# Layer 1 keeps scales and turned quarters of a weight for layer 2, which makes only the sums

## The chip, the cores and the metric

One core of a Trainium2 chip runs the whole program in one launch. The metric is the device time of one execution in microseconds (us); smaller is better. Besides the timed runs there is one profiled execution of the same program, from which all rows below come.

## The reference, cut to what matters

Two attention layers and two gated MLP layers follow each other: `x = x + A(ln(x))`, `x = x + B(ln(x))`, and both once more with the same weights. The change lies in the two B layers, here called layer 1 and layer 2:

```python
def _B_ref(x, w_in, w_sp, b_sp, w_out):            # S = 2048 rows, D = 640, F = 1728, Fh = 864
    z = _gelu(jnp.einsum("bsd,df->bsf", x, w_in))
    z1 = z[..., :Fh]
    z2 = _layernorm(z[..., Fh:], axis=-1)
    g = jnp.einsum("ts,bsf->btf", w_sp, z2) + b_sp[None, :, None]
    return jnp.einsum("bsf,fd->bsd", z1 * g, w_out)
```

`w_sp` (2048 x 2048) multiplies over the sequence, so its rows must be turned (transposed) before TensorE can use them. Both layers use the same `w_sp`.

## The kernel before, in words

All matrix products work on pairs of 16-bit numbers (a high half and the rest, `h` and `l`), three matmuls for one product. A row of `w_sp` is first scaled by a power of two that its largest element gives, then split into `h` and `l` and turned by a transposing DMA.

**Layer 1's spatial product** is in `phase2`. For each of 16 row tiles `t` (128 rows), `rows(t)` loads the 1 MB tile `wr` (one buffer), finds each row's maximum (L577) and scale (`pow2_rows`), and, for each half of the columns, casts the high half on ACT (L587), subtracts on DVE (L588) and turns the result into `wt` by a DMA from the SP queue (L589; two buffers of `wt`). `spatial(t)` runs 96 matmuls over the 16 column blocks (L600) and prepares `u`, which is split and turned to `ut` (L616). `tail` multiplies `ut` by the output weight (`cyp`, L629). TensorE's order is that of the code; a list scheduler sets the order on the other engines and on SP in this phase.

**Layer 2's spatial product** is in `phase2s`. It takes the tiles in eight pairs (256 rows) and cuts the pair's 2 x 2 blocks into quarters a11, a12, a21, a22; seven products of quarter sums replace eight. The sums of `z2` (`zb[0]` to `zb[6]`) are there before. For the weight, `rows(p)` loads the pair's two tiles `wr` (two buffers, L417), finds maximum and scale (L419, `pow2`), scales in place on ACT (L424), and yields seven turned operands in the order in which TensorE uses them: a11, s1 = a21 + a22, s2 = s1 - a11, a12, s3 = a11 - a21, a22, s4 = a12 - s2. The four sums run on POOL (`mix`, L441). Each operand is cast (L431), subtracted (L432) into one of two `wn` buffers and turned (512 KB, L435) into one of eight `wt` buffers. After each product `step` fetches the next operand of the generator, seven ahead.

One pair on TensorE: seven products of 24 matmuls (L458) into the banks `ga` to `gd`, and between them two `tail`s (42 matmuls, `cyp`, L494) of the pair before. After the last product of a tile, `gate` multiplies by `z1` (L473), finds the row maximum (L475), splits on ACT and DVE into the single buffer `un` (L479, L480) and turns it to `ut` (L482). A `tail` waits for that `ut`; its output `xo` (L497) is stored from SP (L498). In `phase2s` both TensorE's and SP's instructions stand in the order of the code; ACT, DVE and POOL are ordered by the scheduler. SP issues every DMA of the kernel, one after the other, and an issue that waits holds back all that stand behind it.

Of the kernel before, what the change touches and what calls it, by code (L numbers as in the profile page):

```python
# [387 lines left out]
def phase2s(g, w_sp, x1_d, z1_d, zb, w0, out):  # L388
# [3 lines left out]
    RING = 8  # L392
    kn = [128] * 6 + [FH - 768]
    ks = [0, 1, 2, 3, 6, 7, 4, 5]
    with ExitStack() as ctx:
        pool = lambda n, b, **k: ctx.enter_context(tc.tile_pool(name=n, bufs=b, reuse_waits="tile", **k))
        pr, ph, ps = pool("dr", 2), pool("dh", 2), pool("ds", 2)
        p1, p2, pv = pool("d1", 1), pool("d2", 2), pool("dv", 1)
        pt = pool("dtr", 1, side="right")
# [3 lines left out]
        cnt, scales = [0], {}  # L403
# [8 lines left out]

        def rows(p):
            w = []
            for t in (2 * p, 2 * p + 1):
                wr = pr.tile([128, S], F32, tag="wr", name="wr")
                nc.sync.dma_start(wr, w_sp[t * 128:(t + 1) * 128, :])  # L417
                am = small("am")
                nc.vector.tensor_reduce(am, wr, AX.X, ALU.max, apply_absolute_value=True)  # L419
                pw, iv = pow2(am, "w", WB)  # L420
                u = g.small.tile([128, 1], F32, tag=f"un{t % 2}", name="un")
                scales.setdefault(p, []).append(u)
                nc.vector.tensor_scalar(u, pw, 1.0 / (WB * ZB), None, ALU.mult)
                nc.scalar.activation(wr, wr, AF.Identity, scale=iv)  # L424
                v = wr.rearrange("p (m i c) -> p i m c", i=2, c=128)
                w.append((v[:, 0], v[:, 1]))

            def turned(src):
                hl = ph.tile([128, 2, 1024], F16, tag="wn", name="wn")
                v = hl.rearrange("p l (m c) -> p l m c", c=128)  # L430
                nc.scalar.copy(v[:, 0], src)  # L431
                nc.vector.tensor_tensor(v[:, 1], src, v[:, 0], ALU.subtract)  # L432
                wt = pt.tile([128, 2, NP, 128], F16, tag=f"wt{cnt[0] % RING}", name="wt")
                cnt[0] += 1
                nc.sync.dma_start(wt.rearrange("p l k c -> p (l k) c"), hl.rearrange("p l c -> p (l c)"), transpose=True)  # L435
                return wt

            def mix(a, b, op, o=None):
                if o is None:
                    o = ps.tile([128, 1024], F32, tag="s", name="s").rearrange("p (m c) -> p m c", c=128)  # L440
                nc.gpsimd.tensor_tensor(o, a, b, op)  # L441
                return o

            (a11, a12), (a21, a22) = w
            yield turned(a11)
            s1 = mix(a21, a22, ALU.add)
            yield turned(s1)
            s2 = mix(s1, a11, ALU.subtract)
            yield turned(s2)
            yield turned(a12)  # L450
            yield turned(mix(a11, a21, ALU.subtract, a21))
            yield turned(a22)
            yield turned(mix(a12, s2, ALU.subtract, a12))
# [7 lines left out]
        def scaled(o, a, un, t):  # L461
            nc.scalar.activation(o, a[:, :FHH], AF.Identity, bias=g.bsp[:, t:t + 1], scale=un)

        def plus(o, a, un, b):
            nc.vector.scalar_tensor_tensor(o, a[:, :FHH], un, b, ALU.mult, ALU.add)
# [6 lines left out]
        def gate(t, u, z1):  # L472
# [4 lines left out]
            hl = p1.tile([128, 2, 128 * KO], F16, tag="un", name="un")  # L477
# [9 lines left out]
        def tail(t, uh, ul, xs, x1=None):  # L487
# [8 lines left out]
            xo = p1.tile([128, 2, 320], F32, tag="xo", name="xo")  # L496
# [3 lines left out]
        todo = (o for p in range(NP) for o in rows(p))  # L500
        with tc.high_priority(offset=HP), ExitStack() as held:
            for i in g.mark:
                held.enter_context(tc.issue_after(i))
            wt = [next(todo) for _ in range(7)]
# [4 lines left out]
        for p in range(NP):  # L509
# [4 lines left out]
            pa, pb, pc, pd = [bank(nm) for nm in "abcd"]  # L514
# [6 lines left out]
            un, un1 = scales[p]  # L521
            step(pa, 0)
            scaled(v, pa, un, t)
            scaled(v1, pa, un1, t + 1)
# [8 lines left out]
            step(pa, 1, False)  # L533
            scaled(u[:, :FHH], pa, un, t)
            step(pb, 5, False)
            plus(q1, pb, un1, v1)
            plus(u1[:, FHH:], pc, un1, q1)
            x1 = [fetch("x1", i, x1_d[i]) for i in (t + 1, t)[:1 + (p + 1 < NP)]] + [None]
            step(pd, 6)
            plus(u1[:, :FHH], pd, un1, q1)  # L540
            pend.append((*gate(t + 1, u1, z1[0]), x1[0]))
            step(pc, 2, False)
            plus(u[:, FHH:], pc, un, q)
            pend.append((*gate(t, u, z1[1]), x1[1]))
        for x in pend:
            tail(*x)


def phase2(g, w_sp, x1_d, z1_d, zh, zl, out, nxt=None):
# [3 lines left out]
    with ExitStack() as ctx:  # L553
# [19 lines left out]
        def rows(t):  # L573
# [4 lines left out]
            pw, iv = pow2_rows(am, "w")  # L578
            un = g.small.tile([128, 1], F32, tag="un", name="un")
            nc.vector.tensor_scalar(un, pw, 1.0 / (WTOP * ZS), None, ALU.mult)  # L580
            ivw = g.small.tile([128, 1], F32, tag="wivw", name="ivw")
            nc.vector.tensor_scalar(ivw, iv, WTOP, None, ALU.mult)
# [829 lines left out]
def interleaved_layers(ctx, tc, x, wq, wk, wv, wo, beta, w_in, w_sp, b_sp, w_out, out):  # L1412
# [68 lines left out]
```

## Time and profile before

| what | value |
|---|---|
| time, median of 3 runs | 2458.88 us (2454.61 to 2461.70) |
| time of the profiled execution | 2444.19 us |
| its span in the profile | 2442.3 us |
| TensorE busy (PE) | 2198.3 us, 90% of the span, 20490 matmuls |
| VectorE (DVE), ScalarE (ACT), GpSimd (POOL) busy | 1554.6, 1197.7, 1066.6 us |
| layer 1's `phase2` on TensorE, first and last spatial matmul | 847.0 to 1233.4 us |
| layer 2's `phase2s` on TensorE, first matmul to last tail | 2016.8 to 2438.2 us |

The profiled execution's time is its span and 1.9 us around it. A row of the timeline has the start, the duration, the engine, the line, the operation, the tiles written and read, the count of merged instructions, and in brackets the idle time of that engine before it and what ended that idle time. PE is TensorE's matmuls, SPq the SP queue's DMA issues. A matmul's recorded duration overlaps the next one's, so that 24 matmuls recorded as 4.54 us follow each other every 4.38 us. Rows of waits have the sum, the count and the longest.

### The profile page before, as it was taken

The page shows a single profiled execution, that of the slowest core. Times are in us where ns is not written, and L with a number is a line of the kernel's source. Part 1 is how long each engine was busy: PE and PEld are TensorE (multiplying, and loading weights), DVE is VectorE, ACT ScalarE, POOL GpSimd, SP SyncE. Part 2 cuts the span into 40 slices and gives each one's busy share as a digit, 9 for nine tenths or more (in the row PEclk, how much of TensorE's full clock was granted, in tenths as well). Part 3 has the DMA queues.
Part 4 walks back from the last instruction along what each step waited for, and adds up shares of the span by engine and source line. Part 5 has one row for each costly group of instructions (what it writes and reads, how often), then busy time and mean ns, then how long its engine had stood idle before and what let it go on. Part 6 is the DMA issues. An engine that isn't in the chain of part 4 may idle for free.

```text
span 2442.3 us, 50615 instructions
## 1 busy us (share of the span) xinstructions
PE 2198.3 (90%) x20490; PEld 1305.8 (53%) x20490; DVE 1554.6 (64%) x2869; ACT 1197.7 (49%) x1476; POOL 1066.6 (44%) x787
## 2 busy tenths in 40 slices
PE   5788899999899899999988989999989987798888
PEld 2454555666455455555544556565655543455454
DVE  7678778776745455444236787887667674555663
ACT  4378688787622322111125987887764242223221
POOL 2178778888510000000004988897863242112320
PEclk9989899999999999999999999999999998899999
DMA  5644545445634488575333263554644327776774
GB/s 164 163 136 102 130 119 137 131 123 146 185 98 128 134 211 199 156 177 145 80 97 89 82 172 100 130 111 127 174 124 114 102 73 182 178 195 151 169 191 106
DMA packets 552426, 337.58 MB, mean 138 GB/s; under 512 B 458432, under 2 KB 493376, under 8 KB 547072
## 3 DMA queue, kind: packets, MB, share of 16 engines
q1 hardware_dynamic: 552192, 334.35, 53.1%
q8 instruction: 161, 2.64, 0.4%
q14 instruction: 73, 0.60, 0.1%
HBM read 148.25 MB, written 85.34 MB: 96 GB/s over the span
## 4 chain that ended last, share of the span: by engine, by line
PE 24%; DMA 8%; DVE 7%; ACT 5%; issue 3%; POOL 2%; SPq 1%; ACTq 0%; DVEq 0%; POOLq 0%
PE zp L308 6%; DMA wt<-wn 2%; PE cyp L494 2%; PE pv L1222 2%; PE yps L979 2%; PE kps L1003 1%; PE gb L458 1%; DMA ut<-un 1%; DVE wn L432 1%; PE mp L1169 1%; PE qps L1003 1%; ACT PH L1195 1%; ACT P L1178 1%; DMA wr<-in_B_w_sp_dram 1%; PE vps L946 1%
## 5 line engine op out<-in xcount | busy, mean ns | idle before, releaser
L1196 POOL TENSOR_TENSOR PL<-P,PH 128x1280 f16<-128x1280 f32 x248 | 650.1, 2623 | 111.3 <-ACT PH L1195 99.6
L1185 DVE TENSOR_REDUCE mx<-mp 128x2 f32<-128x1024 f32 (+3 forms) x512 | 408.8, 817 | 103.9 <-PE mp L1141 102.4
L1178 ACT ACTIVATE P<-es,sc 128x1024 f32<-128x1024 f32 (+1 forms) x384 | 370.7, 965 | 133.0 <-PE es L1141 130.7
L1195 ACT CAST PH<-P 128x1280 f16<-128x1280 f32 x256 | 320.4, 1253 | 20.0 <-PE pv L1222 12.7
L308 PEld LDWEIGHTS <-th 128*128 128x128 f16 x1920 | 187.5, 98 | 176.1 <-issue 8.2
L600 PE MATMUL gp<-zh,wt 128*128 128x432 f16 x1024 | 235.2, 350 | 10.6 <-DMA wt<-wn 10.6
L211 POOL TENSOR_TENSOR lnrs<-lnve,mhalf 128x1 f32<-128x1 f32 x92 | 56.7, 625 | 409.8 <-DVE lnve L210 389.2
L600 PEld LDWEIGHTS <-wt 128*128 128x128 f16 x1536 | 151.8, 99 | 143.8 <-DMA wt<-wn 11.4
L458 PEld LDWEIGHTS <-wt 128*128 128x128 f16 x1344 | 133.4, 99 | 153.3 <-issue 25.2
L1169 PEld LDWEIGHTS <-qk 60*128 60x128 f16 (+1 forms) x2048 | 91.3, 94 | 226.3 <-issue 152.5
L1169 PE MATMUL mp<-qk 60*128 60x512 f16 (+3 forms) x1024 | 138.4, 307 | 42.6 <-DVE mx L1185 41.5
L1222 PE MATMUL pv<-vs,PH 128*128 128x41 f16 x2560 | 167.4, 182 | 1.7 <-DVE ab L1238 1.6
L1141 PEld LDWEIGHTS <-big 64*128 64x128 f16 x3072 | 141.5, 96 | 50.6 <-issue 2.9
L946 PE MATMUL vps<-wvh,xt 128*128 128x320 f16 x640 | 155.6, 310 | 14.0 <-DMA xt<-xnhl 12.0
L1169 PE MATMUL es<-qk 64*128 64x512 f16 (+3 forms) x1024 | 135.1, 299 | 34.9 <-ACT P L1178 23.9
L1222 PE MATMUL pv<-vs,PL 128*128 128x41 f16 x2560 | 163.5, 181 | 1.6 <-POOL PL L1196 1.6
L308 PE MATMUL zp<-wi1h,th 128*128 128x432 f16 x640 | 149.4, 348 | 4.4 <-DMA th<-xnhl 4.3
L1222 PEld LDWEIGHTS <-PH 128*128 128x128 f16 x2560 | 142.3, 96 | 18.6
L615 POOL MEMSET un<- 128x64 f16 x16 | 2.4, 152 | 335.9 <-DMA ut<-un 295.5
L1222 PEld LDWEIGHTS <-PL 128*128 128x128 f16 x2560 | 143.1, 97 | 3.8 <-POOL PL L1196 2.1
L600 PE MATMUL gp<-zl,wt 128*128 128x432 f16 x512 | 137.6, 351 | 0.0
L494 PE MATMUL cyp<-w,ut 128*128 128x320 f16 (+1 forms) x672 | 103.4, 318 | 36.0 <-DMA ut<-un 33.5
(249 smaller groups left out, 4623.4 us busy)
## 6 DMA issues: line engine op xcount, KB each, us to landing
wr<-in_B_w_sp_dram SPq DMA_DIRECT2D x32, 1024.0 KB
qk<-st SPq DMA_DIRECT2D x256, 120.0 KB
x<-x SPq DMA_DIRECT2D x56, 320.0 KB
z<-z SPq DMA_DIRECT2D x32, 432.0 KB
cz<-z SPq DMA_DIRECT2D x32, 432.0 KB
st<-qhl SPq DMA_DIRECT2D x40, 256.0 KB
st<-khl SPq DMA_DIRECT2D x40, 256.0 KB
cx<-x SPq DMA_DIRECT2D x32, 320.0 KB
```

Source lines behind the costliest of these rows:

```text
L308: nc.tensor.matmul(zp[:, n, :FHH], a[:, k, :], b[:, k, c:c + FHH], start=(k == 0 and j == 0), stop=(k == KD - 1 and j == 2))
L458: nc.tensor.matmul(o[:, :FHH], wt[:, x, m, :], zb[b][:, y, m, :], start=start and i == j == 0, stop=i == NP - 1 and j == 2, skip_group_che ...
L494: nc.tensor.matmul(yp[:, n, :320], a[:kn[k], k, :], b[:kn[k], k, n * 320:(n + 1) * 320], start=(k == 0 and j == 0), stop=(k == KO - 1 and ...
L600: nc.tensor.matmul(gp[:, n, :FHH], wt[:, k // 8, a, k % 8, :], b[:, k, n * FHH:(n + 1) * FHH], start=(k == 0 and j == 0), stop=(k == NT - ...
L946: nc.tensor.matmul(ps, a[:, k, c], b[:, k, n * 320:(n + 1) * 320], start=(i == 0), stop=(i == 14))
L1141: nc.tensor.matmul(out, g.big[r, 64 - 64 * s:192 - 64 * s], mk, start=False, stop=s == 1, skip_group_check=True)
L1169: nc.tensor.matmul(out[:, h, o:o + w], a[r, ac], b[r, bc], start=o == 0, stop=False, skip_group_check=True)
L1178: self.last_of["ACT"] = nc.scalar.activation(P[:, :, 512 * c:512 * c + ew], es[:, :, :ew], AF.Exp, scale=g.esc).ins
L1185: self.last_of["DVE"] = nc.vector.tensor_reduce(self.mx[m][:, :, i], mp[:, :, o:o + w], AX.X, ALU.max).ins
L1195: nc.scalar.copy(PH, P[:, h])
L1196: (nc.gpsimd if h == 0 or n < self.N - self.TAIL else nc.vector).tensor_tensor(PL, P[:, h], PH, ALU.subtract)
L1222: nc.tensor.matmul(pv[:, i, h, :], x[:, c:c + 128], v[:, j, h0 + h, :], start=(j == 0 and x is PH), stop=(j == i and x is PL), skip_group_ ...
```

## The change

Layer 1 scales with layer 2's factor (`WB` instead of `WTOP`), splits the columns by alternating blocks of 128 (as layer 2's quarters lie) instead of by halves, keeps each row's scales in the tiles `wpw` and `wiv` (two small POOL copies for each tile), and after each `spatial(t)` stores the turned quarters that layer 2 needs unsummed to DRAM tensors `turned`: both of an even tile (a11, a12), the second of an odd one (a22), 24 stores of 512 KB. Layer 2 finds no maxima and scales any more. It loads a11, a12 and a22 turned from DRAM by plain DMAs, and casts, subtracts and turns only the four sums. `make(n)` makes the operand `n`, `turn(n)` issues its DMA, five operands ahead in a ring of six. `wr` has three buffers, and `rows(p + 1)` is issued after the first product of pair `p`. `un` has two buffers. The seventh product has its own bank `ge`, and its result is added to `u` by a second pass; the two tails stand one product later.

```diff
-    RING = 8
+    RING, AHEAD = 6, 5
-        pr, ph, ps = pool("dr", 2), pool("dh", 2), pool("ds", 2)
+        pr, ph, ps = pool("dr", 3), pool("dh", 2), pool("ds", 2)
...
         def rows(p):
-            w = []
-            for t in (2 * p, 2 * p + 1):
-                wr = pr.tile([128, S], F32, tag="wr", name="wr")
-                nc.sync.dma_start(wr, w_sp[t * 128:(t + 1) * 128, :])
-                am = small("am")
-                nc.vector.tensor_reduce(am, wr, AX.X, ALU.max, apply_absolute_value=True)
-                pw, iv = pow2(am, "w", WB)
...
+            for t in (2 * p + 1, 2 * p):
+                raw[t] = pr.tile([128, S], F32, tag="wr", name="wr")
+                nc.sync.dma_start(raw[t], w_sp[t * 128:(t + 1) * 128, :])
+
+        def scale(p):
+            for t in (2 * p + 1, 2 * p):
+                wr = raw.pop(t)
+                nc.scalar.activation(wr, wr, AF.Identity, scale=g.wiv[:, t:t + 1])
...
+        def make(n):
+            p, b = divmod(n, 7)
+            if p >= NP or b in (0, 3, 5):
+                return
+            if b == 1:
+                scale(p)
+                (a11, a12), (a21, a22) = mixed[2 * p], mixed[2 * p + 1]
+                mixed[p, 1] = src = mix(a21, a22, ALU.add)
...
+            hl = ph.tile([128, 2, 1024], F16, tag="wn", name="wn")
+            v = hl.rearrange("p l (m c) -> p l m c", c=128)
+            nc.scalar.copy(v[:, 0], src)
+            nc.vector.tensor_tensor(v[:, 1], src, v[:, 0], ALU.subtract)
+            split[n] = hl
+
+        def turn(n):
+            p, b = divmod(n, 7)
...
+            wt = pt.tile([128, 2, NP, 128], F16, tag=f"wt{n % RING}", name="wt")
+            if b in (0, 3, 5):
+                nc.sync.dma_start(wt.rearrange("p l k c -> p (l k c)"), g.turned[2 * p + (b == 5)][b > 0])
+            else:
+                nc.sync.dma_start(wt.rearrange("p l k c -> p (l k) c"), split.pop(n).rearrange("p l c -> p (l c)"), transpose=True)
...
-            hl = p1.tile([128, 2, 128 * KO], F16, tag="un", name="un")
+            hl = p2.tile([128, 2, 128 * KO], F16, tag="un", name="un")
...
-            def step(o, b, start=True):
-                product(o, wt.pop(0), b, start)
-                wt.extend(islice(todo, 1))
+            def step(i, o, b, start=True):
+                n = 7 * p + i
+                product(o, ready.pop(n), b, start)
+                turn(n + AHEAD)
+                if i == 0:
+                    rows(p + 1)
+
+            def then(i):
+                make(7 * p + i + AHEAD + 1)
...
-            step(pc, 3)
-            if pend:
-                tail(*pend.pop(0))
-            step(pb, 4)
-            plus(q, pb, un, v)
+            step(1, pc, 3)
+            then(1)
+            step(2, pb, 4)
+            plus(q, pb, t, v)
+            plus(u[:, FHH:], pc, t, q)
+            then(2)
+            if pend:
+                tail(*pend.pop(0))
+            step(3, pa, 1, False)
+            scaled(u[:, :FHH], pa, t)
+            then(3)
             if pend and p + 1 < NP:
                 tail(*pend.pop(0))
...
-            step(pc, 2, False)
-            plus(u[:, FHH:], pc, un, q)
+            step(6, pe, 2)
+            plus(u[:, FHH:], pe, t, u[:, FHH:])
             pend.append((*gate(t, u, z1[1]), x1[1]))
+            then(6)
...
+        def store(t, wt):
+            for i in range(t % 2, 2):
+                nc.sync.dma_start(g.turned[t][i], wt[0][:, i].rearrange("p l k c -> p (l k c)"))
...
-                        nc.tensor.matmul(gp[:, n, :FHH], wt[:, k // 8, a, k % 8, :], b[:, k, n * FHH:(n + 1) * FHH],
+                        nc.tensor.matmul(gp[:, n, :FHH], wt[:, k % 2, a, k // 2, :], b[:, k, n * FHH:(n + 1) * FHH],
...
             u = spatial(t, wt)
+            store(t, wt)
             wt = rows(t + 1) if t + 1 < NT else None
```

Three places show how the instructions stand now. The first is SP in layer 2, from the loads of the next pair's rows to the first `ut` of the running pair: before,

```order
L417 DMA wr<-in_B_w_sp_dram 128x2048 x2
L435 DMA_TRANSPOSE wt<-wn 128x16x128 x2
L498 DMA out_dram<-xo 128x640
L435 DMA_TRANSPOSE wt<-wn 128x16x128
L498 DMA out_dram<-xo 128x640
L469 DMA cz_30374<-z_1_9 128x864
L469 DMA cz_30376<-z_1_8 128x864
L435 DMA_TRANSPOSE wt<-wn 128x16x128 x2
L469 DMA cx_30440<-x_1_9 128x640
L469 DMA cx_30442<-x_1_8 128x640
L435 DMA_TRANSPOSE wt<-wn 128x16x128
L482 DMA_TRANSPOSE ut<-un 128x14x128
```

and the same stretch now (the first turned operand is s4 of the running pair, the next two s1 and s2 of the next pair):

```order
L422 DMA wr<-in_B_w_sp_dram 128x2048 x2
L467 DMA_TRANSPOSE wt<-wn 128x16x128
L465 DMA wt<-turned_0 128x2048
L513 DMA out_dram<-xo 128x640
L467 DMA_TRANSPOSE wt<-wn 128x16x128
L513 DMA out_dram<-xo 128x640
L484 DMA cz_30302<-z_1_9 128x864
L484 DMA cz_30304<-z_1_8 128x864
L467 DMA_TRANSPOSE wt<-wn 128x16x128
L484 DMA cx_30334<-x_1_9 128x640
L484 DMA cx_30336<-x_1_8 128x640
L465 DMA wt<-turned_1 128x2048
```

Behind it follow `ut`, the turned s3, the second `ut` and a plain load of a22, and then the next `wr`: three of seven transposing DMAs became plain loads, and the second output's store now stands between s1 and s2.

The second place is DVE in a middle pair, from the splits (`wn`) to the first gate (`u<-u,cz`): before,

```order
L432 TENSOR_TENSOR wn<-wr,wn 128x1024
L432 TENSOR_TENSOR wn<-s,wn 128x1024 x2
L465 SCALAR_TENSOR_TENSOR q_30548<-gb,un,v_30546 128x432
L465 SCALAR_TENSOR_TENSOR u<-gc,un,q_30548 128x432
L497 SCALAR_TENSOR_TENSOR xo<-cyp,xs,cx_30442 128x640
L432 TENSOR_TENSOR wn<-wr,wn 128x1024
L465 SCALAR_TENSOR_TENSOR u<-gd,un,q_30548 128x432
L432 TENSOR_TENSOR wn<-wr,wn 128x1024
L473 TENSOR_TENSOR u<-u,cz_30761 128x864
```

and now:

```order
L456 TENSOR_TENSOR wn<-s,wn 128x1024 x2
L456 TENSOR_TENSOR wn<-wr,wn 128x1024
L512 SCALAR_TENSOR_TENSOR xo<-cyp,xs,cx_30336 128x640
L480 SCALAR_TENSOR_TENSOR q_30440<-gb,unt,v_30438 128x432
L480 SCALAR_TENSOR_TENSOR u<-gc,unt,q_30440 128x432
L456 TENSOR_TENSOR wn<-wr,wn 128x1024
L480 SCALAR_TENSOR_TENSOR u<-gd,unt,q_30440 128x432
L488 TENSOR_TENSOR u<-u,cz_30662 128x864
```

The third split (s3, `wn<-wr`) stands ahead of the second `xo`, and the fourth (s4) ahead of `u<-gd`, with which the first gate of the pair begins.

The third place is ACT where layer 2's first pair begins: before,

```order
L431 CAST wn<-s 128x1024
L431 CAST wn<-wr 128x1024 x2
L462 ACTIVATE v<-ga,bsp,un 128x432
L462 ACTIVATE v_28703<-ga,bsp,un 128x432
L431 CAST wn<-wr 128x1024 x2
```

(a11 and s1 were cast further up), and now:

```order
L363 CAST zb_26770<-zt_28604 128x432
L477 ACTIVATE v<-ga,bsp,unt 128x432
L477 ACTIVATE v_28730<-ga,bsp,unt 128x432
L455 CAST wn<-s 128x1024 x2
L455 CAST wn<-wr 128x1024 x2
```

All four casts of the first pair stand behind `v`, which reads the first product.

More of the change, by code (lines that the diff above doesn't have):

```diff
@@ L411, in pow2 @@
             return pw, iv
+        un = g.small.tile([128, NT], F32, tag="unt", name="unt")
+        nc.vector.tensor_scalar(un, g.wpw, 1.0 / (WB * ZB), None, ALU.mult)
+        un = [un[:, t:t + 1] for t in range(NT)]
+        raw, mixed, split, ready = {}, {}, {}, {}
         def rows(p):
[L414 to L426 removed]
@@ L438, in mix @@
[L438 to L450, printed above, removed]
@@ L451, in rows @@
-            yield turned(mix(a11, a21, ALU.subtract, a21))
-            yield turned(a22)
-            yield turned(mix(a12, s2, ALU.subtract, a12))
+            if p >= NP:
+                return
[6 more added lines that the diff above has]
+                nc.scalar.activation(wr, wr, AF.Identity, scale=g.wiv[:, t:t + 1])
+                v = wr.rearrange("p (m i c) -> p i m c", i=2, c=128)
+                mixed[t] = v[:, 0], v[:, 1]
@@ L503, in phase2s @@
                 held.enter_context(tc.issue_after(i))
-            wt = [next(todo) for _ in range(7)]
+            rows(0)
+            for n in range(AHEAD + 1):
+                make(n)
+                if n < AHEAD:
+                    turn(n)
         woh, wol = g.wu.place(w0)
@@ L1417, in interleaved_layers @@
     g.bsp = cp.tile([128, NT], F32, tag="bsp", name="bsp")
+    g.wpw = cp.tile([128, NT], F32, tag="wpw", name="wpw")
+    g.wiv = cp.tile([128, NT], F32, tag="wiv", name="wiv")
     attn_consts(g, cp, beta)
@@ L1428, in interleaved_layers @@
     g.st = [dram(f"st{i}", (D, 3, 2, L), F16) for i in range(2)]
+    g.turned = [[dram(f"turned{t}_{i}", (128, 2048), F16) for i in range(2)] for t in range(NT)]
     kept = kept_tiles(g, ats)
```

77 lines of the change are left out of this document (43 added, 34 removed).

## The prediction

> **What bounds the kernel now.** I read the stages first (busy times of the engines in windows), then who TensorE waits for in the last stage, then its timeline there, and last the other engines' rows in one pair. Layer 1's spatial stage, once under way, from the windows; the columns are the window, its length, the busy times of PE, weight load, DVE, ACT, POOL, the clock, the DMA share and GB/s:
>
> ```profile
> 892.00:1233.00 341.00, 337.75 (x2014) 197.34 (x2012) 143.23 (x256) 61.88 (x64) 9.88 (x22) 0.99 0.61 149
> ```
>
> PE is busy for 337.75 of 341 us at 0.99 of full clock: TensorE bounds this stage, and whatever delays it there is lost for good. Layer 2's stage (2016 to 2443) is different. PE's waits there (sum in us, times, longest):
>
> ```profile
> PE cyp L494 <- DMA ut<-un: 33.5, 6, 13.2
> PE ga L458 <- DMA wt<-wn: 19.0, 2, 14.4
> PE gc L458 <- DVE u L465: 14.5, 8, 4.3
> ```
>
> Together 67 us: the tails wait for the gate's turned `ut`, and pairs 0 and 1 for their turned a11. PE's timeline shows where:
>
> ```profile
> 2006.60 5.64 PE L308 MATMUL zp<-w,th 128*128 128x432 f16 x30
> 2016.84 6.08 PE L458 MATMUL ga<-zb,wt 128*128 128x432 f16 x24 [4.60 <-DMA wt<-wn]
> 2022.76 4.54 PE L458 MATMUL gc<-zb,wt 128*128 128x432 f16 x24
> 2027.13 4.54 PE L458 MATMUL gb<-zb,wt 128*128 128x432 f16 x24
> 2044.65 4.54 PE L458 MATMUL gc<-zb,wt 128*128 128x432 f16 x24
> 2063.59 6.59 PE L458 MATMUL ga<-zb,wt 128*128 128x432 f16 x24 [14.39 <-DMA wt<-wn]
> 2087.73 7.79 PE L494 MATMUL cyp<-w,ut 128*128 128x320 f16 x42 [13.17 <-DMA ut<-un]
> 2099.73 5.87 PE L494 MATMUL cyp<-w,ut 128*128 128x320 f16 x42
> 2197.71 5.87 PE L494 MATMUL cyp<-w,ut 128*128 128x320 f16 x42
> 2228.91 4.54 PE L458 MATMUL gc<-zb,wt 128*128 128x432 f16 x24 [1.68 <-DVE u L465]
> 2237.78 7.55 PE L494 MATMUL cyp<-w,ut 128*128 128x320 f16 x42 [4.33 <-DMA ut<-un]
> 2289.00 7.84 PE L494 MATMUL cyp<-w,ut 128*128 128x320 f16 x42 [5.21 <-DMA ut<-un]
> 2389.14 7.27 PE L494 MATMUL cyp<-w,ut 128*128 128x320 f16 x42 [4.59 <-DMA ut<-un]
> 2400.64 4.54 PE L458 MATMUL ga<-zb,wt 128*128 128x432 f16 x24
> 2432.36 5.87 PE L494 MATMUL cyp<-w,ut 128*128 128x320 f16 x42 [1.49 <-DVE xo L497]
> ```
>
> A product takes 2027.13 - 2022.76 = 4.37 us, a tail 5.71 (5.87 as recorded, less the overlap of 0.16), so a pair is 7 x 4.37 + 2 x 5.71 = 42.0 us of TensorE. But the first tails of pairs 1 and 7 begin 2389.14 - 2087.73 = 301.4 us apart, 50.2 a pair. From 2237.78 on the wait in each pair is 4.3 to 5.2 us, and it costs more than itself: that tail is recorded as 7.55 to 7.84 us and not 5.87, some 1.7 us at a lower clock. After 1.68 us of idling (2228.91) the product is not longer.
>
> What makes PE wait is a loop through the other engines, seen from SP, DVE, ACT and POOL in one pair:
>
> ```profile
> 2240.07 1.53 SPq L482 DMA_TRANSPOSE ut<-un  x1
> 2241.64 1.51 SPq L417 DMA_DIRECT2D wr<-in_B_w_sp_dram  x2
> 2247.68 2.29 DVE L419 TENSOR_REDUCE am<-wr 128x1 f32<-128x2048 f32 x1 [1.42 <-DMA wr<-in_B_w_sp_dram]
> 2253.32 3.90 ACT L424 ACTIVATE wr<-wr,wiv 128x2048 f32<-128x2048 f32 x2 [14.47 <-DVE wiv L410]
> 2257.30 2.35 POOL L441 TENSOR_TENSOR s<-wr 128x1024 f32<-128x1024 f32 x1 [13.00 <-ACT wr L424]
> 2260.76 3.26 DVE L432 TENSOR_TENSOR wn<-s,wn 128x1024 f16<-128x1024 f32 x1
> 2260.80 5.29 SPq L435 DMA_TRANSPOSE wt<-wn  x2
> 2265.35 1.05 ACT L431 CAST wn<-s 128x1024 f16<-128x1024 f32 x1 [4.01 <-DMA wt<-wn]
> 2266.43 1.23 DVE L432 TENSOR_TENSOR wn<-s,wn 128x1024 f16<-128x1024 f32 x1 [2.40 <-ACT wn L431]
> 2271.86 8.13 SPq L435 DMA_TRANSPOSE wt<-wn  x2
> 2279.99 1.04 ACT L431 CAST wn<-wr 128x1024 f16<-128x1024 f32 x1 [6.80 <-DMA wt<-wn]
> 2289.06 1.01 ACT L479 ACTIVATE un<-u,uiv 128x864 f16<-128x864 f32 x1 [4.96 <-DMA ut<-un]
> ```
>
> The next pair's rows (`wr`) are asked for only behind the second `ut` of the last one (2240.07, then 2241.64). Six us later the first has landed (2247.68), two maxima of 2.3 us follow, the scaling at 2253.32, the first sum at 2257.30, then seven turns through two `wn` buffers; a cast waits each time for a turned operand to land (2265.35, 2279.99). The last `ut` needs the single `un` buffer, and ACT waits for it until the first `ut` has landed (2289.06). Then the next `wr` can be asked for, some 50 us after the last. This loop, not TensorE, sets the pair's time.
>
> **The change part by part.** I follow TensorE from layer 1 to the end.
>
> *Layer 1, the start.* Rows of the first two tiles on PE and SP:
>
> ```profile
> 846.97 0.90 PE L600 MATMUL gp<-zh,wt 128*128 128x432 f16 x2 [7.39 <-DMA wt<-wn]
> 849.39 0.50 SPq L575 DMA_DIRECT2D wr<-in_B_w_sp_dram  x1
> 870.60 0.90 PE L600 MATMUL gp<-zh,wt 128*128 128x432 f16 x2 [3.18 <-DMA wt<-wn]
> ```
>
> Column blocks now alternate between the two halves of `wt`, so the second matmul group needs the second turned half, while before it was wanted only at the ninth block, 8.7 us later. Two turned halves land one transfer apart; a transfer is priced below at 2.8 us, so a wait of 1 to 3 us comes for tile 0 and for tile 1. On SP the two stores of tile 0 wait until both halves have landed and then stand ahead of tile 1's `wr` (849.39); they bring 1 MB into the DMA engines, 2.7 us. PE waited for tile 1 already (870.60), so both delays reach it: 2.7 + 2.5, **+5 us**; ends 2 and 12 (the second if the stores also hold up the output weight's split behind them). Behind tile 1 PE never waits for `wt` in this trace, and a `ut` is asked for a whole tile (23 us) ahead of its tail, so the other 22 stores, some 5 us of SP's waiting a tile, stay hidden; the cover gone is the third rival. The POOL copies and the strided splits lie beside an idle POOL and DVE: nothing.
>
> *What a turned operand costs against a plain load.* Two windows, in the first almost only transposing DMAs, in the second plain loads of long rows:
>
> ```profile
> 2012.30:2016.80 4.50, 0.00 (x0) 0.00 (x0) 4.07 (x5) 2.28 (x4) 2.57 (x2) 0.97 0.82 154
> 2037.00:2046.00 9.00, 9.00 (x51) 4.85 (x50) 1.34 (x2) 0.00 (x0) 0.00 (x0) 1.00 1.00 386
> ```
>
> 154 GB/s at a share of 0.82 are 188 GB/s at full share, against 386: 512 KB (524 kB) take 2.8 us turned and 1.4 us plain. From issue to landing a lone turn takes 4.55 (2260.80 to the cast at 2265.35), behind two loads of `z1` 8.1 (2271.86 to 2279.99). The plain loads of a11, a12 and a22 hang on nothing but a free ring place, so only their transfer counts. [...]
>
> *Layer 2, pairs 0 and 1.* PE ends the stage before at 2006.60 + 5.64 = 2012.24. Now a11 is a plain load without a cast and can lie ready: the first product starts at once and not at 2016.84. But no s1 exists then. Its sum writes into memory of the stage before, whose last store SP now issues at about 2013.5 (its activation's end), so I put POOL's start at 2016; sum 2.35, cast 1.05 (behind `v`, as the third place shows), split 2.5 (between 1.23 at 2266.43 and 3.26 at 2260.76, beside POOL), turn 4.55: landed at 2026.5. **PE waits 10 us** at its second product and loses 1.7 to the clock; six more products end at 2054.5, where before the last ended at 2044.65 + 4.54 = 2049.2, so 5 us behind. Then the two big waits of before go (14.4 for a11, 13.2 for `ut`). Pair 1's rows are asked for at 2033, behind the output weight; 4.6 MB at 386 GB/s land by 2046.5. Scaling 1.95 (half of 2253.32's row), cast and split 3.55, turn 4.55: s1 at 2056.6, before PE asks for it at 2059. DVE comes to the pair's two gates when s3 is split (2.3 more), finishes them with two products, two maxima, s4's split and the rest by 2069, and `ut` lands at 2073. PE has done a, c and b by 2054.5 + 13.1 = 2067.6, waits 5, and ends the tail at 2073 + 5.7 + 1.7 = 2080.4. Before, the same products and tail were done at 2099.73: **19 us ahead**.
>
> *The loop now.* From one issue of `wr` to the next, with these rows for the durations of gates and outputs:
>
> ```profile
> L475 DVE TENSOR_REDUCE uam<-u 128x1 f32<-128x864 f32 x16 | 16.7, 1049 | 0.3
> L480 DVE SCALAR_TENSOR_TENSOR un<-u,uiv,un 128x864 f16<-128x864 f32 x16 | 17.8, 1114 | 30.3 <-ACT un L479 30.3
> L497 DVE SCALAR_TENSOR_TENSOR xo<-cyp,xs,cx 128x640 f32<-128x640 f32 x16 | 14.1, 883 | 53.3 <-PE cyp L494 42.5 <-DMA out_dram<-xo 10.8
> ```
>
> Second `wr` landed: 6.0 + 2.7 for its 1 MB + 1.4 for the a22 in front = 10.1. Scaling 1.95. Cast and split of s1 3.55. Turn 4.55. Now the second and first place bite: SP's store of the second output stands between s1 and s2, its `xo` stands on DVE behind the split of s3, and that cast waits for s1 to land and free its `wn`: cast 1.05, split 1.23, `xo` 0.88, three issues 1.4 = 4.6. Turn of s2 behind the `z1` loads 8.1. Cast and split of s4 2.3, which DVE does ahead of `u<-gd`; then both gates one after the other: two `plus` 1.3, two products 2.1, two maxima 2.1, two splits 2.2, ACT 1.0, scalars 0.8 = 11.8 with s4. Issue of `ut` and a22 2.0. Sum 46.6, and some 1.4 for twenty handovers: **48 us a pair**. The maxima and three of seven turns went, and `un`'s second buffer saves its wait, but the loop still passes through `ut`, `wr` and two landings, and is longer than TensorE's 42.0. PE then waits about 4.5 us at each first tail, the clock's 1.7 lies beside the loop, and the added bank and later tails move nothing. Ends: 45 with short turns of s2 (6 us), 52 if SP or the DMA engines hold each turn up by 1 us more.
>
> Only in pair 1 does DVE's order put the second `xo` ahead of s2's split, without the detour: that pair runs at 42.
>
> *The sum.* From 2080.4, a pair of 42 and one of 48 reach 2170.4, where before stood 2197.71: 27 ahead. The next four, (2400.64 - 2197.71) / 4 = 50.7 before, are 48: 11 more. The last products and three tails (to 2432.36) hang on the same gates as before: nothing. -38 + 5 = **-33 us**. The profiled execution would be 2444.2 - 33 = 2411; the runs' median lies at 2458.9, so 2426.
>
> **The rivals.** *The loop no longer binds.* If the turn of s2 is short and DVE comes early to the gate, PE's 42 us set the pair. For it: a lone turn is 4.55, and the engines are far from busy. Against: the detour is in the order of two queues and cannot be skipped. Five pairs x 6 = 30 us less: 2396. Chance 0.10.
>
> *The loop stays as long as it was.* Issues of turns were held on SP up to 8.1 us for two (2271.86); if a backlog of `wr` and plain loads adds 4 us a pair, the loop is 52: five pairs x 4 = 20 more, 2446. For it: the DMA engines move as many bytes in less time. Against: turned bytes, the slow ones, fall from nine to six a pair. Chance 0.13.
>
> *Slower: layer 1's stores reach TensorE.* SP holds at each store until its halves have landed, and `ut` and the next `wr` stand behind. If a tile's 4.55 us came through in full, 16 x 4.55 = 73, and the time would be 2426 + 73 - 5 = 2494. It decides from (38 + 7) / 16 = 2.8 us a tile. For it: PE has no slack there (337.75 of 341). Against: one tile is 23 us, and the chain from `wr` to landed `wt` needs no more than the 21 us from 849.39 to 870.60, with other loads in between. Chance 0.06.
>
> **How the numbers follow.** My forecast has 0.69, and 0.02 are left for what I don't see. The range, 2402 to 2448, takes in the loop's ends of 45 and 52 (five pairs: -15 and +20) and layer 1's 2 to 12, and leaves out the first rival and the slower one. A change under 0.3% (7.4 us) cannot be told from none here. Faster by more: the forecast, the first rival and most of the second, 0.88; within it 0.05; slower 0.07.
>
> **What would show it.** Right: PE's second product of pair 0 starts near 2026 + 5, the first tails of pairs 3 to 7 wait 4 to 5 us for `ut` and lie 48 us apart, the tail of pair 2 does not wait, and in layer 1 PE waits for `wt` only in tiles 0 and 1. Wrong in size: tails 42 or 52 apart. Wrong altogether: waits for `wt` or `ut` in layer 1 behind tile 2, or the loads of `turned` as what PE waits for.

## The result, and the profile after

The changed kernel takes 2415.97 us (median of 4 runs, 2414.56 to 2419.65) against 2458.72 us before: a ratio of 0.983 (95% interval 0.9811 to 0.9848), 42.7 us less. The forecast was 2426 in a range of 2402 to 2448. The profiled execution took 2419.65 us, its span 2417.8.

TensorE's waits in layer 2's spatial stage after the change (sum, times, longest):

```profile
PE cyp L509 <- DMA ut<-un: 21.7, 6, 5.0
PE gc L473 <- DMA wt<-wn: 11.7, 1, 11.7
PE cyp L509 <- DVE xo L512: 2.0, 2, 1.0
```

The 67 us of waiting, 69.5 with 2.5 for `xo`, are 35.4, and 0.4 in one short wait for `wt`. TensorE's timeline shows where they stand now:

```profile
2022.05 5.64 PE L308 MATMUL zp<-w,th 128*128 128x432 f16 x30
2027.53 4.54 PE L473 MATMUL ga<-zb,wt 128*128 128x432 f16 x24
2043.75 7.31 PE L473 MATMUL gc<-zb,wt 128*128 128x432 f16 x24 [11.68 <-DMA wt<-wn]
2091.81 8.48 PE L509 MATMUL cyp<-w,ut 128*128 128x320 f16 x42 [5.02 <-DMA ut<-un]
2136.51 5.87 PE L509 MATMUL cyp<-w,ut 128*128 128x320 f16 x42
2181.92 7.55 PE L509 MATMUL cyp<-w,ut 128*128 128x320 f16 x42 [3.17 <-DMA ut<-un]
2228.86 5.88 PE L509 MATMUL cyp<-w,ut 128*128 128x320 f16 x42 [3.02 <-DMA ut<-un]
2321.71 7.55 PE L509 MATMUL cyp<-w,ut 128*128 128x320 f16 x42 [2.87 <-DMA ut<-un]
2369.19 7.55 PE L509 MATMUL cyp<-w,ut 128*128 128x320 f16 x42 [3.55 <-DMA ut<-un]
```

The first product starts at once. The second, on s1, waits 11.7 us. The first tail of pair 1 waits for `ut`, that of pair 2 doesn't, and those of pairs 3 to 7 wait 2.9 to 4.1 us and lie (2369.19 - 2181.92) / 4 = 46.8 us apart, where they lay 50.2 apart before. From the end of the stage before (2027.69) to the end of the span the stage takes 390.1 us; before, it took 2442.3 - 2012.24 = 430.1. So layer 2 won 40.0 us.

Layer 1 lost. From TensorE's first rows there, and SP's ahead of the last one:

```profile
854.30 0.90 PE L638 MATMUL gp<-zh,wt 128*128 128x432 f16 x2 [0.22 <-DMA wt<-wn]
877.49 0.90 PE L638 MATMUL gp<-zh,wt 128*128 128x432 f16 x2 [4.73 <-DMA wt<-wn]
881.31 0.90 PE L638 MATMUL gp<-zh,wt 128*128 128x432 f16 x2 [1.49 <-DMA wt<-wn]
941.40 1.10 SPq L628 DMA_DIRECT2D turned<-wt  x1
942.55 0.96 SPq L606 DMA_DIRECT2D wr<-in_B_w_sp_dram  x1
944.73 3.77 SPq L225 DMA_TRANSPOSE xt<-xnhl  x1
948.60 3.54 SPq L654 DMA_TRANSPOSE ut<-un  x1
954.21 0.71 PE L667 MATMUL cyp<-wuh,ut 128*128 128x320 f16 x2 [7.83 <-DMA ut<-un]
```

Tiles 0 and 1 wait for the second turned half too, as forecast. Then one tail waits 7.83 us for a `ut` that SP asked for only at 948.60, 6 us ahead of it and right behind a transposing prefetch of the next stage (`xt`). Counted between the same two matmuls of TensorE's unchanged order (the 8000th and the 10500th, from 818.3 to 1270.7 us, and before from 813.5 to 1257.7), layer 1 takes 8.2 us more. The rest of the difference of the two profiles, 2442.3 - 2417.8 = 24.5 = 40.0 - 8.2 - 7.3, lies in stages that the change doesn't touch; the last experiment speaks of it.

### The profile page after: what moved, and what is told of

Same layout as the page of the kernel before. It is cut to its first block, busy times and chain, and to the rows that moved or that the text cites. A ratio compares the mean times of both kernels' runs of the same rounds, so it can differ in the third digit from the quotient of the medians.

```text
span 2417.8 us, 50515 instructions
## 1 busy us (share of the span) xinstructions
PE 2203.2 (91%) x20490; PEld 1306.8 (54%) x20490; DVE 1491.6 (62%) x2758; ACT 1173.1 (49%) x1452; POOL 1072.1 (44%) x819
## 5 line engine op out<-in xcount | busy, mean ns | idle before, releaser
L1208 PE MATMUL es<-qk 64*128 64x512 f16 (+3 forms) x1024 | 135.9, 301 | 34.3 <-ACT P L1217 23.6
L1042 PE MATMUL kps<-xt,wkh 128*128 128x512 f16 x380 | 123.4, 394 | 9.5 <-DVE phl L1076 9.4
```

The source lines that it names most:

```text
L1042: nc.tensor.matmul(ps, a[:, k, c], b[:, k, :], start=(i == 0), stop=(i == 14))
L1208: nc.tensor.matmul(out[:, h, o:o + w], a[r, ac], b[r, bc], start=o == 0, stop=False, skip_group_check=True)
```

## The experiments

Medians of 4 or more runs each, but for the last; the changed kernel stands at 2416.0 us.

**The late store.** The second output's store and the loads of `z1` go behind s2's turn:

```diff
             then(3)
-            if pend and p + 1 < NP:
-                tail(*pend.pop(0))
-            z1 = [fetch("z1", i, z1_d[i]) for i in (t + 1, t)]
+            put = tail(*pend.pop(0), late=True) if pend and p + 1 < NP else None
             step(4, pb, 5, False)
+            if put:
+                put()
+            z1 = [fetch("z1", i, z1_d[i]) for i in (t + 1, t)]
```

> The changed kernel, but the store of a pair's second output and the loads of z1 are issued behind the turn of s2 and not ahead of it. Theory (the loop through s2's turn sets the pair): in the changed kernel s2's split ended at 2296.3 and its turn was issued at 2302.0, because the queue stood at the store; 5.7 us of the 46.8 us a pair go, the loop falls to about 41, TensorE's 42.0 bound instead, and five pairs win 4.8 us each: 2416 - 24 = 2392 us, and the waits for ut at the first tails of pairs 3 to 7 (2.9 to 4.1 us) are gone or under 1 us. Rival (the DMA engines' bytes set the pair, and a turn asked for earlier lands no earlier): 2416 us, with waits as before.

Measured 2393.82 us (2393.0 to 2396.32). The first tails of pairs 2 and 7, and TensorE between them (a window; columns as in the prediction):

```profile
2135.23 5.87 PE L509 MATMUL cyp<-w,ut 128*128 128x320 f16 x42
2345.62 5.87 PE L509 MATMUL cyp<-w,ut 128*128 128x320 f16 x42
2100.00:2345.00 245.00, 245.00 (x1462) 142.85 (x1461) 126.10 (x165) 71.69 (x66) 69.40 (x37) 1.00 0.84 212
```

(2345.62 - 2135.23) / 5 = 42.1 us a pair, and PE is busy for 245 of 245 us at full clock. What bound the changed kernel in pairs 3 to 7 was the place of one store and two loads on a queue, not the amount of any work: this kernel has the same instructions. The pair moves the same bytes in less time, 212 GB/s at a share of 0.84, so the rival falls.

**Seven turns, and seven with three copies.** The first makes a11, a12 and a22 in layer 2 again; the second does so too, but moves these three by a plain copy:

```diff
-            if p >= NP or b in (0, 3, 5):
-                return
-            if b == 1:
-                scale(p)
+            if p >= NP:
+                return
+            if b == 0:
+                scale(p)
+            if b in (0, 3, 5):
+                src = mixed[2 * p + (b == 5)][b > 0]
+            elif b == 1:
...
             if b in (0, 3, 5):
-                nc.sync.dma_start(wt..., g.turned[2 * p + (b == 5)][b > 0])
+                nc.sync.dma_start(wt..., split.pop(n)..., transpose=True)    # seven turns
+                nc.sync.dma_start(wt..., split.pop(n)...)                    # three copies
```

> The changed kernel (kept scales, no maxima, two un buffers, three wr buffers, new places), but a11, a12 and a22 are cast, split and turned in layer 2 again instead of loaded; layer 1 still stores them. Theory (three turns, with their casts and their two wn buffers, are the larger part of what the loop lost, as the maxima alone brought a loop of 49.9 instead of 50.2): the loop is 50 us again, and pair 0 waits for a11 too: 2416 + 6 x 3.2 + 5 = 2440 us or more. Rival (the places and the buffers brought the gain, and turns ride along): 2416 us.

> The kernel that makes all seven operands in layer 2 again (2446 us), but a11, a12 and a22, still cast and split there, go from wn to wt by a plain copy of the same 512 KB and not by a transposing DMA: it leaves out the turning of these three. Theory A (a turned operand is slow in the DMA engines and in its queue, 2.8 us of transfer against 1.4, three a pair): most of the 30 us come back, 2416 to 2425 us. Theory B (what costs is that seven operands instead of four pass ACT, DVE and two wn buffers, each waiting for an earlier one to land): 2440 us or more.

Measured 2446.14 us (2443.68 to 2453.64) and 2428.57 us (2426.93 to 2431.21). The first tails of pairs 3 and 7, of the seven turns and then of the three copies:

```profile
2202.68 7.65 PE L509 MATMUL cyp<-w,ut 128*128 128x320 f16 x42 [10.34 <-DMA ut<-un]
2402.32 8.51 PE L509 MATMUL cyp<-w,ut 128*128 128x320 f16 x42 [6.32 <-DMA ut<-un]
```

```profile
2188.96 8.25 PE L512 MATMUL cyp<-w,ut 128*128 128x320 f16 x42 [4.58 <-DMA ut<-un]
2380.86 7.55 PE L512 MATMUL cyp<-w,ut 128*128 128x320 f16 x42 [3.55 <-DMA ut<-un]
```

Pairs of 49.9 and of 48.0 us. The three loads are worth 30.2 us in all. Of these, 17.6 (2446.1 - 2428.6) come from the transposing alone; the other 12.6 belong to the casts, the splits and the passage through two `wn` buffers together, which no run takes apart. Neither theory holds by itself: A carries some six tenths.

**Scales only.** The kernel before, with layer 1's scales used in layer 2 and all seven operands turned there:

```diff
-                nc.vector.tensor_reduce(am, wr, AX.X, ALU.max, apply_absolute_value=True)
-                pw, iv = pow2(am, "w", WB)
...
-                nc.scalar.activation(wr, wr, AF.Identity, scale=iv)
+                nc.scalar.activation(wr, wr, AF.Identity, scale=g.wiv[:, t:t + 1])
```

> The kernel before, with layer 1's scales kept and used in layer 2: no maxima there. Layer 1 splits by alternating blocks but stores nothing; layer 2 still makes and turns all seven operands, and its places, banks and buffers are those of before. Theory (in the loop of 50.2 us each pair waits for two maxima behind the rows' landing): the scaled rows are ready about 4.5 us earlier, the loop is 46 us, six pairs and pair 1's start win 4.5 us each, layer 1 loses 4: 2459 - 30 + 4 = 2433 us. Rival (the seven turns with two wn buffers are the bound, and earlier rows only wait longer for a buffer): 2459 + 4 = 2463 us.

Measured 2451.18 us (8 runs, 2447.19 to 2453.24), ratio 0.9973 (0.9962 to 0.9983): 6.5 us won, not 26. One pair on SP, ACT and DVE:

```profile
2249.65 1.56 SPq L420 DMA_DIRECT2D wr<-in_B_w_sp_dram  x2
2260.53 8.58 SPq L433 DMA_TRANSPOSE wt<-wn  x2
2264.63 5.70 DVE L430 TENSOR_TENSOR wn<-s,wn 128x1024 f16<-128x1024 f32 x2 [4.18 <-ACT wn L429]
2269.16 0.92 SPq L496 DMA_DIRECT2D out_dram<-xo  x1
2273.14 0.89 DVE L495 SCALAR_TENSOR_TENSOR xo<-cyp,xs,cx 128x640 f32<-128x640 f32 x1 [2.81 <-DMA out_dram<-xo]
2274.05 0.34 SPq L496 DMA_DIRECT2D out_dram<-xo  x1
2299.59 1.58 SPq L420 DMA_DIRECT2D wr<-in_B_w_sp_dram  x2
```

The first turn is issued 10.9 us after the rows were asked for, and not 19.2 (2241.64 to 2260.80 before): the maxima did stand in the way. But the next rows are asked for 49.9 us after these, not 51.2. The row of the first two turns is 8.58 us long and not 5.29: the second turn waits for the split of s1, which DVE begins 4.1 us after the first turn's issue (2264.63) and not together with it (2260.76 before). The first output's store stands behind the two, and the second `xo` waits 2.81 us for that store's landing, since it has one buffer. From the first turn to the second store it takes 13.5 us instead of 9.4, and from there to the next rows 25.5 instead of 22.7: some 7 of the 8.3 us are given back behind the first turn. Layer 1 takes a part too: between the two matmuls used above it takes 446.9 us (818.8 to 1265.7) instead of 444.2, with the alternating blocks and without a store.

**One `un` buffer, and the old places.** One undoes `p2` to `p1` for `un`; the other puts the seventh product back into `gc` and both tails one product earlier.

```diff
-            hl = p2.tile([128, 2, 128 * KO], F16, tag="un", name="un")
+            hl = p1.tile([128, 2, 128 * KO], F16, tag="un", name="un")
```

> The changed kernel with one un buffer instead of two, as before the change. Theory (loop): the second gate's activation waits again until the first ut has landed, about 4 us behind its issue instead of 0.7, so the loop gets 3 to 4 us longer in each of the six pairs that it binds: 2416 + 20 = 2436 us. Rival (the second buffer is idle weight, since the turns of one queue come one after the other anyway): 2416 us.

```diff
+            if pend:
+                tail(*pend.pop(0))
             step(2, pb, 4)
             plus(q, pb, t, v)
-            plus(u[:, FHH:], pc, t, q)
             then(2)
-            if pend:
+            if pend and p + 1 < NP:
                 tail(*pend.pop(0))
...
-            step(6, pe, 2)
-            plus(u[:, FHH:], pe, t, u[:, FHH:])
+            step(6, pc, 2, False)
+            plus(u[:, FHH:], pc, t, q)
```

> The changed kernel with the seventh product in bank gc again and the two tails one product earlier, where they stood before the change; all else as changed. Theory (the loop of the queues sets the pair, not where the tails stand): each first tail comes 4.4 us earlier to a ut that lands when it did, so it waits longer but the pair takes no longer; the second output's store now stands ahead of s1's turn and no longer holds s2's, so the loop gets up to 4 us shorter: 2395 to 2416 us. Rival (the later tails and the own bank are a part of the gain): each of seven pairs loses the 4.4 us of a product: 2416 + 31 = 2447 us.

Measured 2421.45 us (2419.26 to 2423.28) and 2410.09 us (2407.21 to 2416.40). With one buffer the second gate's activation waits for the first `ut`'s landing again (ACT, below), 4.3 us, but with two it had waited 1.6 us for its scalars, and the pairs from the fourth on (PE) are (2367.98 - 2223.23) / 3 = 48.2 us instead of 46.8: right in sign, a quarter of the size. The runs of the two kernels just touch, and the longer pairs speak for a real difference.

```profile
2319.62 1.02 ACT L494 ACTIVATE un<-u,uiv 128x864 f16<-128x864 f32 x1 [4.27 <-DMA ut<-un]
2223.23 7.55 PE L509 MATMUL cyp<-w,ut 128*128 128x320 f16 x42 [3.62 <-DMA ut<-un]
2367.98 7.49 PE L509 MATMUL cyp<-w,ut 128*128 128x320 f16 x42 [4.50 <-DMA ut<-un]
```

With the old places the first tails of pairs 3 and 7 lie 45.2 us apart:

```profile
2178.58 5.88 PE L509 MATMUL cyp<-w,ut 128*128 128x320 f16 x42 [0.50 <-DMA ut<-un]
2359.24 5.88 PE L509 MATMUL cyp<-w,ut 128*128 128x320 f16 x42 [1.22 <-DMA ut<-un]
```

So the own bank and the later tails, by themselves, likely cost some 6 us: the runs of the two kernels overlap (2407.21 to 2416.40 against 2414.56 to 2419.65), but the pairs are 1.6 us shorter. With the old places the second output's store stands ahead of s1's turn, and s2's turn is issued 22.9 us after the rows (2272.52 to 2295.37) instead of 23.6 (2278.39 to 2302.00). That is half of the 1.6; where the other half lies was not followed.

**Layer 1 alone, and its stores on another queue.** Layer 1 as changed with layer 2 as before; and the kernel with the late store, with layer 1's stores issued from ScalarE:

```diff
-                nc.sync.dma_start(g.turned[t][i], wt[0][:, i].rearrange("p l k c -> p (l k c)"))
+                nc.scalar.dma_start(g.turned[t][i], wt[0][:, i].rearrange("p l k c -> p (l k c)"))
```

> Layer 1 as changed (alternating column blocks, kept scales, 24 stores of turned quarters), layer 2 as before: what is stored is not read. Theory (layer 1 costs what the two profiles show, 3.8 us at tiles 0 and 1 and a 7.8 us wait for ut at tile 3, in all 8 us): 2459 + 8 = 2467 us. Rival (the wait at tile 3 was chance): 2459 + 4 = 2463 us. Rival (the stores reach TensorE in every tile): 2459 + 45 or more.

> The kernel with the late store, and layer 1's 24 stores are issued from ScalarE's queue instead of SyncE's. Theory (the stores cost layer 1 time because SyncE's queue holds at them, with ut and the next rows behind): the wait of 6 to 8 us for ut at tile 3 goes, and with it some of tile 1's: 2394 - 8 = 2386 us. Rival (it is their 12.6 MB in the DMA engines): 2394 us.

Measured 2467.01 us (2463.12 to 2468.24), 9.3 more than before, as the theory has it: the wait at tile 3 is no chance, it comes again with 7.8 us. And 2396.02 us (2395.28 to 2400.42): nothing won, and TensorE still waits 7.44 us at this tile. With no store left in SP's queue, its `ut` is asked for no earlier, right behind the same prefetch:

```profile
942.90 6.79 SPq L225 DMA_TRANSPOSE xt<-xnhl  x1
949.80 3.36 SPq L656 DMA_TRANSPOSE ut<-un  x1
```

So the time for which SP itself *holds* at the stores isn't the main cause. Two delays add up. In the changed kernel `un` was split at 940.58 + 1.12 = 941.70 and its `ut` went out only at 948.60, with the prefetch as the longest of what stood ahead (3.77 us, the two stores 0.40 and 1.10); in the kernel before, `un` was split at 926.87 and `ut` went out at 927.12. And `un` is late itself, since rows come late: those of tile 3 took 9.3 us from their issue to their maxima (897.51 to 906.79), 10.2 with the stores on ScalarE (896.81 to 906.99), but at most 6.0 before (888.46 to 894.45) and 6.1 with the stores behind the rows (898.55 to 904.65, in the last kernel below). This agrees with the stores' transfer ahead of the rows as a cause; how much of the wait each delay makes, no run separates.

**The first pair, the halves, and stores behind the rows.** Three steps on top of the late store, each with the one before in it: in pair 0 the products with loaded operands first and pair 1's first row tile loaded early; in layer 1 even column blocks ahead of odd ones; layer 1's stores behind the next tile's loads and turns.

```diff
-            for n in range(AHEAD + 1):
+            for n in (0, 5, 3, 1, 2, 4):
...
+            if p == 0:
+                product(pa, ready.pop(0), 0)
...
+                product(pd, ready.pop(5), 6)
+                turn(6)
+                rows(1, 1, 2)
+                z1 = [fetch("z1", i, z1_d[i]) for i in (t + 1, t)]
+                product(pa, ready.pop(3), 1, False)
...
-            for k in range(NT):
+            for k in (*range(0, NT, 2), *range(1, NT, 2)):
...
-            store(t, wt)
-            wt = rows(t + 1) if t + 1 < NT else None
+            old, wt = wt, rows(t + 1) if t + 1 < NT else None
+            store(t, old)
```

> The kernel with the late store, and in pair 0 the three products with loaded operands (a11, a22, a12) first, s1 to s4 behind them; pair 1's row tile with a21 and a22 is loaded before the first pair's turns, and z1 of pair 0 ahead of pair 1's turns. Theory (pair 0 waits 11.7 us only because s1 cannot be made before the stage before lets go of its memory): two products of 4.4 us more lie ahead of the wait, which falls to about 3 us and a quarter of the clock's loss, and the first tail no longer waits 6.4 us: 2394 - 16 = 2378 us. Rival (what is saved in pair 0 is waited for in pair 1, whose s1 and s2 need rows that can be loaded no earlier): 2390 to 2394 us.

> The kernel with the first pair's loaded products first, and in layer 1 TensorE takes the even column blocks first and the odd ones behind them, so that the second turned half is wanted at the ninth block again. Theory (a part of layer 1's loss is the wait of the second matmul group for the second half): the waits for wt there fall from 14.4 to the 10.6 us of the kernel before, 2383 - 4 = 2379 us. Rival (the second half lands so late only because the DMA engines are full, and then the ninth block waits): 2383 us.

> The same, with layer 1's stores of a tile issued behind the loads and turns of the next tile's rows and not ahead of them. Theory (the rest of layer 1's loss is the stores' place ahead of the next rows and of ut): the wait of 6 to 8 us for ut at tile 3 goes back to the 3 us or less of the kernel before, and tile 1's wait for wt falls from 5.6 to 3.2: 2379 - 6 = 2373 us. Rival (it is the stores' bytes, wherever they stand): 2379 us.

Measured 2383.16 (2381.73 to 2384.98), 2379.28 (2375.38 to 2383.43) and 2375.28 us (2371.07 to 2376.96). The first pair wins 10.7 of the 16: its one wait of 11.7 us is now a handful in pairs 0 and 1, the longest of 2.8 and 2.7 us (for s4 and s1). The two steps in layer 1 win about 4 us each, where 4 and 6 were expected; at each step the runs of the two kernels overlap, so each gain is likely and not sure. The traces agree: between the two matmuls used above, layer 1 takes 452.3, 448.7 and 446.6 us in the three kernels. In the last step tile 1 waits 1.34 us (at 873.48) instead of 5.58 (at 879.25), and the `ut` at tile 3 is waited for 4.48 us instead of 6.20, not the 3 us or less of the theory.

The last one is the fastest version here, at a ratio of 0.9673 to the kernel before (0.9653 to 0.9694) and 40.7 us below the changed kernel.

**Before, once more.**

> The kernel before, profiled a second time, since its first profiled execution took 2444.2 us and its timed runs 2450 to 2463. If the difference lies ahead of layer 2's spatial stage, that stage again takes some 430 us from TensorE's end of the stage before to the end of the span; if it lies within, 440 us or more, and layer 2 won more by the change than the 40 us of the two profiles.

It took 2454.55 us, its span 2452.7, and TensorE's last matmuls ahead of layer 2's stage are these:

```profile
2013.90 5.64 PE L308 MATMUL zp<-w,th 128*128 128x432 f16 x30
```

The stage takes 2452.7 - 2019.54 = 433.2 us, against 430.1 in the first profile; the other 7.3 us of the difference lie ahead of it. By this profile layer 2 won 43.1 us. The kernel with layer 1 alone has the same layer 2 too. Its span is 2466.5 us, and the same matmuls stand here:

```profile
2024.59 5.64 PE L308 MATMUL zp<-w,th 128*128 128x432 f16 x30
```

There the stage takes 2466.5 - 2030.23 = 436.3 us. Three profiles of one layer 2 thus spread over 6 us, and they place its gain between 40 and 46 us.

## Why the prediction was right, point by point

Sign, mechanism and place were right; the time came out 10 us lower than forecast.

- **The base.** The sum of -33 was laid on a profiled execution of 2444.2 us and carried over to the median. Between the profiles the parts that it speaks of gave -40.0 + 8.2 = -31.8, with the second profile of before -34.9, and with layer 2 from the kernel with layer 1 alone -38.0. So the sum came near, but in part by luck. By the first profiles it was too hopeful for layer 1 (by 3.2 us) and for pairs 0 and 1 (by 4.4) and too cautious for the pairs behind them (25.1 us won against 19), and these errors cancel. The medians differ by 42.7; where the rest of that lies stays open.
- **Layer 1, +5: measured +8.2.** Tiles 0 and 1 lost about 4, as worked out. The step that failed is "a `ut` is asked for a whole tile (23 us) ahead of its tail": that was read from the waits, not from the rows. In the kernel before, this same `ut` was issued 10.4 us ahead of its tail, and TensorE did wait for the next one:

```profile
927.12 5.95 SPq L616 DMA_TRANSPOSE ut<-un  x1
937.48 0.43 PE L629 MATMUL cyp<-wuh,ut 128*128 128x320 f16 x2
964.12 0.45 PE L629 MATMUL cyp<-wuh,ut 128*128 128x320 f16 x2 [3.25 <-DMA ut<-un]
```

  Now later turns, two stores and a prefetch stand ahead of it. As in the third rival the stores reach TensorE, at one tile of sixteen, but through the late rows and the prefetch more than by SP's holding at a store. A wait for `ut` behind tile 2 was named as a sign of being "wrong altogether", and it came; the sign was badly chosen, since a wait of 3.25 us for a `ut` stood in the kernel before, and this one is only 4.6 us longer. Of the 8.2 us the alternating blocks alone make 2.7 (scales only), which leaves 5.5 for the stores.
- **Pairs 0 and 1, 19 ahead: measured 15.** The first tail ends at 2100.29, which is 2084.8 on the clock of the profile before, and not 2080.4. The second product waited 11.7 us instead of 10 and ran 2.8 us longer instead of 1.7 (granted clock 0.50 in the window 2043.90:2047.20, 0.72 in 2047.20:2051.00). Pair 1's rows were asked for at 2052.41, which is 2037.0 there and not 2033, because SP stood at pair 0's turns (5.15 us from 2039.43, 3.58 from 2046.13); s1, the gates and `ut` follow them. (The prediction's own sum is off here too: 2033 and 11.9 us for 4.6 MB at 386 GB/s make 2044.9, not 2046.5.)
- **The loop, 48 us: measured 46.8.** One pair on SP, ACT and DVE:

```profile
2278.39 0.91 SPq L422 DMA_DIRECT2D wr<-in_B_w_sp_dram  x2
2293.07 2.02 SPq L467 DMA_TRANSPOSE wt<-wn  x1
2297.44 1.04 ACT L455 CAST wn<-wr 128x1024 f16<-128x1024 f32 x1 [3.82 <-DMA wt<-wn]
2299.66 0.88 DVE L512 SCALAR_TENSOR_TENSOR xo<-cyp,xs,cx 128x640 f32<-128x640 f32 x1
2302.00 3.83 SPq L467 DMA_TRANSPOSE wt<-wn  x1
2307.98 1.04 ACT L455 CAST wn<-wr 128x1024 f16<-128x1024 f32 x1 [9.49 <-DMA wt<-wn]
2319.28 1.12 DVE L495 SCALAR_TENSOR_TENSOR un<-u,uiv,un 128x864 f16<-128x864 f32 x1 [1.13 <-ACT un L494]
2324.90 0.91 SPq L422 DMA_DIRECT2D wr<-in_B_w_sp_dram  x2
```

  To s1's turn 14.7 us (15.6 reckoned), its landing 4.4 (4.55), to s2's turn 4.6 (4.6), its landing 6.0 (8.1), s4 and both gates 12.4 (11.8), and from there to the next rows 4.5 (2.0, since s3's turn stands between the two `ut`s and was not counted). The sum is 46.5, as reckoned without handovers. The first term came near by luck: the prediction counted to the second row tile and left out POOL's sum, but s1 needs only the tile that is loaded first, scaled from 2284.06 on and summed by POOL from 2286.14 on (2.35 us). The late store shows that this chain set the pair, and that no other held it above TensorE's own 42.1. The waits at the tails were 2.9 to 4.1 us, not 4.5. The recorded length of such a tail before was also misread: not 7.55 to 7.84 us, but 7.27 (2389.14) to 8.36 (2339.15). The lower clock shows in windows behind the start of two of them: 0.58 in 2237.90:2241.20, 0.50 in 2289.10:2292.40.
- **What each part was worth.** Undone one at a time, the plain loads brought 30 of the 43 us and the second `un` buffer 5.5. "The added bank and later tails move nothing" was likely wrong: by themselves they cost some 6. And the maxima, counted as gone from the loop, won only 6.5 by themselves (scales only): what the first turn gained was mostly lost again on s1's split and a store, which the prediction's walk along one chain does not see. What the maxima are worth once the three turns are gone, no run shows.
- **The rivals.** That the loop no longer binds, forecast as 2396, needed one more edit and then gave 2393.8. A loop of 52 us did not come; it was 46.8.

## What to carry to other kernels

Where one queue issues everything, write down for each pair what stands between a transfer that others wait for and its issue: moving one store and two loads behind a turn won 22 us here with no work taken away. Shortening one chain tells its worth only if no second one of the same length runs beside it, so undo the parts one by one before you credit them. Before you call a transfer hidden, look up its issue row and its reader's row in the stage at hand; an engine that never waited tells nothing of how near it was.

## What was not expected of the hardware

In the kernel with the old places, two products of one kind waited 2.08 and 2.20 us:

```profile
2209.78 6.22 PE L473 MATMUL gc<-zb,wt 128*128 128x432 f16 x24 [2.08 <-DVE u L480]
2344.72 4.54 PE L473 MATMUL gc<-zb,wt 128*128 128x432 f16 x24 [2.20 <-DVE u L480]
```

The first then ran 1.7 us longer, the second did not. Windows behind the two give the granted clock (third figure from the end):

```profile
2209.80:2213.20 3.40, 3.40 (x12) 1.48 (x12) 1.02 (x1) 1.04 (x1) 0.00 (x0) 0.58 0.99 321
2344.80:2348.00 3.20, 3.20 (x18) 1.67 (x18) 0.00 (x0) 0.99 (x1) 0.00 (x0) 1.00 1.11 281
```

In the changed kernel the tail behind a wait of 2.87 us is longer (2321.71, 7.55 us; granted clock 0.60 in the window 2321.80:2325.10) and that behind one of 3.02 us isn't (2228.86, 5.88 us; 1.00 in 2228.90:2232.20). So the length of a wait doesn't decide alone, and one of 2.1 us can be enough. What else decides, no run shows.

A transposing DMA issued right behind the two loads of rows held SP for 7.85 us, where others in the same pair held it 2.0 and 3.8 (2293.07, 2302.00):

```profile
2279.40 7.85 SPq L467 DMA_TRANSPOSE wt<-wn  x1
```

No row shows that it cost anything here: s1, next in the queue to be waited for, was split only at 2293.
